# A transformer block on one core: order lists written out, tile 0's second centring behind tile 2's statistics, tile 1 copied by ScalarE alone

## The chip, the core and the metric

The kernel runs on one core of a Trainium2 chip. Its engines have queues of their own and meet through semaphores: TensorE (PE; its weight loads are PEld), VectorE (DVE), ScalarE (ACT), GpSimd (POOL) and SyncE (SP), which issues DMAs here. The metric is the device time of one execution in microseconds, the median of the runs; smaller is better.

## The reference

```python
x: (1, 2048, 512)   w1, w2: (512, 512)   w3: (512, 1792)   w4: (1792, 512)   all bf16
h   = gelu(layernorm(x) @ w1)              # tanh form
g0..g3 = the four 128-column quarters of h, shifted along the tokens
         by 1 down, 1 up, 2 down, 2 up, with zeros at the ends
x1  = x + concat(g0, g1, g2, g3) @ w2
out = x1 + gelu(layernorm(x1) @ w3) @ w4
```

## The kernel before

The 2048 tokens are 16 tiles of 128. A first layer (layernorm, w1, gelu) gives `hT`, transposed, with the tokens along the row, so that the shifted quarters are only other slices of it. `mix` multiplies them by w2 and adds x. A second layer (layernorm, w3, gelu, w4) gives the output. Everything stays on the chip between.

Each piece of work is an `Op` with a name, an engine and the resources that it reads and writes. Below, q is the tile for layer 1 and 16 + tile for layer 2:

- **Statistics** (lines 407 to 440). On VectorE `bnst` (batch-norm statistics of a tile, L432) and `bnag` (their aggregate, L434). For tiles in `STAT_ACT` ScalarE takes the sums instead (`sum`, L411, and `ssq`, L416; in layer 2 the sum falls out of the addition), and VectorE finishes with `mean`, `msq` (L424) and `vpe` (L428, which reads two small tensors). GpSimd then makes `rstd` (L439).
- **Normalizing**, `norm`: on VectorE (L461, from mean and rstd), or on ScalarE (L470) or GpSimd (L473), for which `nmr` (L466), minus mean times rstd, is made first. `NORM` chooses the engine, `NMR` that of nmr. Tile 0 is only centred (L448), in two halves `norm0_0` and `norm0_1`, and its rstd is applied later, inside its gelu.
- **Transposing.** Tiles 0 to 7 of layer 1 are transposed by TensorE (L506) and copied from PSUM to `xnT` (`ev`, L514); `EVAC` says by ScalarE, VectorE, or one half each ("both"). All others go through a DMA transpose that SP issues (`tp`, L479).
- **Matmuls.** `rows0` for tile 0 (L544) with `gelur0` and a transpose back, `th0`, copied by `evh0`; `up1` and `up2` (L642) for groups of 1, 2 or 4 tiles (`GROUPS`), in blocks of at most 1024 PSUM columns, each followed by a gelu on ScalarE (L657); `mix` (L697), followed by `x1`, the addition on VectorE (L709 or L713); `down` (L731), followed by `res` (L739) and the output's DMA.

PSUM is divided in two. `y_ps` is three pairs of banks, taken in turn by up, rows0 and the transposes called `ty` in the script. `o_ps` is two banks, taken in turn by mix, down, th0 and the transposes called `tp` in the script. A bank is taken again when its reader is done.

TensorE's order is the one of `SCRIPT` (lines 290 to 295). The other four engines' orders come out of a planner: `order()` works out a due time for each op from written-in costs (`dur`, `HOP`, `BIAS`), and `place()` plays the program through with them and lets each engine take the most urgent op that is ready. `LOADS` gives the order of the DMA loads and of two of the DMA transposes among them. `emit` (L811) writes the instructions and waits in that order; the ops planned ahead of 1900 ns stand ahead of the entry barrier.

The orders that came out, as far as 26 us, by engine:

```
SP    x0 x2 w1a w1b x3 x4 w2b w2a x6 x7 x8 w3 x12 x11 tp16 tp17 x14 tp9 tp8 tp10 tp11 tp12
ACT   sum0 ssq0 ev0_0 ev0_1 ev1act gelur0 sum5 gelu1_1 ssq5 gelu1_2 sum7 ev3 norm5 ssq7 gelu1_3 sum9 ev6act norm7 ...
DVE   bnst1 bnag1 norm0_0 norm0_1 bnst2 norm1 bnag2 msq0 vpe0 norm2 ev1dve bnst3 ev2 bnag3 bnst4 evh0 norm3 bnag4
      msq5 vpe5 bnst6 norm4 bnag6 x1_0 ev4 msq7 x1_1 ev5 vpe7 bnst16 ev6dve bnag16 bnst17 bnag17 norm16 x1_2 norm17
      msq9 vpe9 ev7 bnst8 x1_3 bnag8 bnst11 norm8 msq10 vpe10 bnag11 x1_5 nmr10 msq12 nmr11 vpe12 bnst13 bnag13 x1_4 ...
POOL  rstd1 rstd2 rstd0 rstd3 rstd4 rstd5 nmr5 rstd6 nmr6 norm6 rstd7 nmr7 rstd16 rstd17 rstd9 nmr9 norm9 rstd8 rstd10
      rstd11 norm10 rstd12 rstd13 nmr12 rstd15 nmr15 rstd14 norm15 ...
```

Of the kernel before, what the change touches and what calls it, by code (L numbers as in the profile page):

```python
# [6 lines left out]
P = 128  # L7
# [7 lines left out]
class Op:  # L15


    def __init__(self, name, eng, fn, reads, writes, dur, queue):
        self.name, self.eng, self.fn = name, eng, fn
        self.reads, self.writes = list(reads), list(writes)  # L20
        self.dur, self.queue = dur, queue
        self.idx = 0
        self.descs = 8.0
        self.prio = 1e9
        self.first = None

class Program:

    HOP = {"pe": 200.0, "dve": 155.0, "act": 220.0, "pool": 120.0, "sp": 70.0}
    LOOK = {"dve": 300.0, "act": 300.0}
    DUE = 179877.0
    BEGIN = {"sp": 30.0, "act": 150.0, "pe": 400.0, "dve": 150.0, "pool": 450.0}
    ENTRY = 1900.0
    COLD, RESTART = 4300.0, 800.0
    RING = 150.0
    LAG = {"load": 750, "tp": 350}

    def __init__(self):  # L40
        self.ops = []
        self.lines = []

    def add(self, eng, name, fn, reads=(), writes=(), dur=100.0, queue=None):
        op = Op(name, eng, fn, reads, writes, dur, queue)
        op.idx = len(self.ops)
        self.ops.append(op)
        return op

    def line(self, names):  # L50

        self.lines.append(list(names))

    def order(self):
# [25 lines left out]
        order_only = set()  # L80
        for names in self.lines:
            for a, b in zip(names, names[1:]):
                assert named[a].eng == named[b].eng, (a, b)
                order_only.add((named[a].idx, named[b].idx))
        last = None
        pe_pos = 0
        for op in self.ops:
            if op.eng == "pe":
                if last is not None:
                    preds[op.idx].add(last.idx)  # L90
                last = op
                op.prio = pe_pos
                pe_pos += 1
        order_only = {(a, b) for a, b in order_only if a not in preds[b]}
        for a, b in order_only:
            preds[b].add(a)
        succs = [set() for _ in self.ops]
        for i, d in enumerate(preds):
            for j in d:
                succs[j].add(i)  # L100
        left = [len(s) for s in succs]
        stack = [i for i, n in enumerate(left) if n == 0]
        seen = 0
        while stack:
            i = stack.pop()
            seen += 1
            for j in preds[i]:
                if self.ops[j].eng != "pe":
                    self.ops[j].prio = min(self.ops[j].prio, self.ops[i].prio)
                left[j] -= 1  # L110
                if left[j] == 0:
                    stack.append(j)
        assert seen == len(self.ops), "cycle"
        if self.DUE:

            topo, left = [], [len(d) for d in preds]
            stack = [i for i, n in enumerate(left) if n == 0]
            while stack:
                i = stack.pop()
                topo.append(i)  # L120
                for j in succs[i]:
                    left[j] -= 1
                    if left[j] == 0:
                        stack.append(j)
            due, t = {}, self.DUE
            for op in self.ops:
                if op.eng == "pe" and not op.name.startswith("warm"):
                    due[op.idx] = t
                    t += op.dur
            for i in reversed(topo):  # L130
                op = self.ops[i]
                late = due.get(i, 1e9)
                for j in succs[i]:
                    o = self.ops[j]
                    hop = 70.0 if op.queue else (self.HOP[op.eng] if o.eng != op.eng else 120.0)
                    work = (2300.0 if op.queue == "tp" else op.dur + 1850.0) if op.queue else op.dur
                    late = min(late, o.prio - hop - work)
                op.prio = late
        for op in self.ops:
            op.prio += BIAS.get(op.name, 0.0)  # L140
            if op.first is not None:
                op.prio = op.first
        for names in self.lines:
            for a, b in reversed(list(zip(names, names[1:]))):
                named[a].prio = min(named[a].prio, named[b].prio - 1e-3)

        self.preds = preds
        out = self.place(succs, order_only)
        for a, b in order_only:
            preds[b].discard(a)  # L150
        return out

    def place(self, succs, order_only):

        npend = [len(d) for d in self.preds]
        ready = [0.0] * len(self.ops)
        cands = {e: [] for e in ENGINES}
        for op in self.ops:
            if npend[op.idx] == 0:
                cands[op.eng].append(op)  # L160
        free = dict(self.BEGIN)
        rings = {"sp": [], "act": []}
        fed = {}
        clock = moved = last = turned = self.total = 0.0
        out = []

        def finish(limit):
            nonlocal clock
            while True:
                heads = {e: r[0] for e, r in rings.items() if r}  # L170
                if not heads:
                    return None
                live = [e for e in heads if heads[e][0] <= clock]
                later = min([h[0] for h in heads.values() if h[0] > clock], default=1e18)
                if not live:
                    if later > limit:
                        return None
                    clock = later
                    continue
                first = min(live, key=lambda e: heads[e][1])  # L180
                step = heads[first][1] * len(live)
                ends = clock + step <= min(later, limit)
                if not ends:
                    step = min(later, limit) - clock
                for e in live:
                    heads[e][1] -= step / len(live)
                clock += step
                if ends:
                    return rings[first].pop(0)[2]
                if clock >= limit:  # L190
                    return None

        def release(op, o, at):
            npend[o.idx] -= 1
            if at is not None:
                ready[o.idx] = max(ready[o.idx], at)
            if npend[o.idx] == 0:
                cands[o.eng].append(o)

        def land(op):  # L200
            nonlocal moved, last, turned
            if op.queue == "tp":
                turned = max(clock + 500.0, op.start + 2450.0, last + 500.0, turned + 480.0)
                at = turned + self.LAG["tp"]
            elif op.name.startswith("out"):
                at = clock + 300.0
                self.total = max(self.total, at)
            else:
                moved += op.dur
                at = clock + 600.0 + min(600.0, 0.3 * moved) + (600.0 if op.dur > 1400.0 else 0.0)  # L210
                at += 50.0 if moved <= 1200.0 else self.LAG["load"] - 300.0 if moved <= 4000.0 else self.LAG["load"] if moved <= 11000.0 else self.LAG["load"] + 650.0
            if op.queue != "tp":
                last = max(last, at)
            op.landed = at
            for j in succs[op.idx]:
                if (op.idx, j) not in order_only:
                    release(op, self.ops[j], at + 30.0)

        while len(out) < len(self.ops):
            while True:  # L220
                best = None
                for e in ENGINES:
                    if cands[e]:
                        t = max(free[e], min(ready[o.idx] for o in cands[e]))
                        if best is None or t < best[0]:
                            best = (t, e)
                op = finish(best[0] if best else 1e17)
                if op is None:
                    break
                land(op)  # L230
            t, e = best
            look = self.LOOK.get(e, 1.0)
            op = min((o for o in cands[e] if ready[o.idx] <= t + look), key=lambda o: (o.prio, o.idx))
            cands[e].remove(op)
# [674 lines left out]
```

## Time and profile before

| | |
|---|---|
| median of 3 runs | 135.43 us (134.98 to 135.43) |
| span of the profiled execution | 133.73 us from its first to its last instruction |
| its whole time, if it was a median run | 135.43 us: 1.70 us lie around the span |
| TensorE busy | 130.6 us, 98% |
| VectorE, ScalarE, GpSimd busy | 50.9, 56.0, 30.9 us |
| granted TensorE clock | 1.00 in all stretches |
| first transpose of tile 1 (tp1) | 5.12 us |
| first up2 block | 19.06 us |
| last matmul's result added | 131.96 us |
| DMA | 12.19 MB, mean 91 GB/s |

The page gives the busy time of each engine, then the span in 40 slices of 3.3 us, each with the busy share in tenths. The chain of work that ended last is followed back from the last instruction: its pieces say who set the time at each moment. The timeline lists instructions with start, length, engine, line and tiles. The starts of neighbouring instructions of one engine tell its pace better than their lengths do, since instructions overlap by a tenth of a microsecond.

### The profile page before, as it was taken

The numbers are of one execution on the slowest core, as the hardware profiler recorded it, in microseconds if no ns is written. First come the engines' busy times: TensorE is split into PE (matmuls) and PEld (weight loads), VectorE is DVE, ScalarE is ACT, GpSimd is POOL, SyncE is SP. The second block draws the span as 40 slices with busy tenths as digits, with TensorE's granted clock in tenths as the row PEclk, the third lists the DMA queues.
The fourth block names the chain that finished last, engine by engine and source line by source line (L and its number), as shares of the span: only waits on it lengthen the run. The fifth ranks groups of instructions, "written<-read, shape, count | busy, mean of one in ns | idle before, by whom it ended". The sixth has DMA issues, their size and how long they took to land.

```text
span 133.7 us, 2004 instructions
## 1 busy us (share of the span) xinstructions
PE 130.6 (98%) x776; PEld 71.8 (54%) x789; DVE 50.9 (38%) x138; ACT 56.0 (42%) x89; POOL 30.9 (23%) x69
## 2 busy tenths in 40 slices
PE   8999999999999999999999999999999999999994
PEld 3488768874488444444444444444444444444464
DVE  1899998887550830052260003322220000232223
ACT  5699998858657155520025553000006663000000
POOL 2447567696544120012022003100000000000000
PEclk9999999999999999999999999999999999999999
DMA  4999966745442991002211000311111000111112
GB/s 134 329 349 401 237 150 95 83 89 107 98 99 49 295 329 40 0 0 43 77 42 39 0 0 0 78 39 44 39 42 37 0 0 0 39 44 39 39 39 78
DMA packets 21305, 12.19 MB, mean 91 GB/s; under 512 B 13872, under 2 KB 20784, under 8 KB 21296
## 3 DMA queue, kind: packets, MB, share of 16 engines
q1 hardware_dynamic: 20864, 11.93, 32.7%
q10 hardware_dynamic: 432, 0.13, 0.4%
q8 instruction: 6, 0.10, 0.3%
q14 instruction: 3, 0.02, 0.1%
HBM read 6.82 MB, written 2.10 MB: 67 GB/s over the span
## 4 chain that ended last, share of the span: by engine, by line
PE 94%; DMA 2%; DVE 2%; issue 1%; SPq 0%
PE y_ps L642 46%; PE o_ps L731 36%; PE o_ps L697 10%; DMA x_sb<-in_x_dram 2%; PE y_ps L506 1%; DVE st L432 1%; PE y_ps L544 1%; DVE xn_buf L448 0%; DVE xn_buf L461 0%; DVE o_sb L739 0%; PE o_ps L610 0%; DVE mv L434 0%; SPq L894 0%
## 5 line engine op out<-in xcount | busy, mean ns | idle before, releaser
L642 PE MATMUL y_ps<-xnT,w_sb 128*128 128x512 bf16 (+2 forms) x421 | 63.6, 308 | 0.2
L642 PEld LDWEIGHTS y_ps<-xnT,w_sb 128*128 128x128 bf16 x424 | 38.4, 98 | 24.6 <-DVE mv L434 0.2
L731 PE MATMUL o_ps<-w_sb,h2T 128*128 128x512 bf16 (+3 forms) x248 | 48.7, 355 | 0.2
L657 ACT ACTIVATE h2T<-y_ps 128x1024 bf16<-128x1024 f32 (+1 forms) x29 | 28.6, 993 | 47.2 <-PE y_ps L642 47.1
L731 PEld LDWEIGHTS o_ps<-w_sb,h2T 128*128 128x128 bf16 x252 | 23.6, 98 | 25.2
L739 DVE TENSOR_TENSOR o_sb<-o_ps,x_sb 128x512 bf16<-128x512 f32 (+3 forms) x18 | 11.4, 632 | 45.7 <-PE o_ps L731 45.7
L439 POOL TENSOR_TENSOR rstd<-mv,neghalf 128x1 f32<-128x1 f32 x20 | 11.1, 553 | 35.1 <-DVE mv L434 30.1
L697 PE MATMUL o_ps<-w_sb,hT 128*128 128x512 bf16 x58 | 14.8, 379 | 0.3
L432 DVE BATCH_NORM_STATS2 st<-x_sb 128x6 f32<-128x512 bf16 x20 | 13.5, 676 | 2.6 <-DMA x_sb<-in_x_dram 2.5
L713 DVE TENSOR_TENSOR x_sb<-o_ps,x_sb 128x512 bf16<-128x512 f32 x10 | 6.8, 677 | 14.8 <-PE o_ps L697 14.8
L439 POOL TENSOR_TENSOR rstd<-vpe,neghalf 128x1 f32<-128x1 f32 x12 | 6.7, 558 | 15.6 <-DVE vpe L428 15.5
L473 POOL TENSOR_SCALAR xn_buf<-x_sb,rstd,nmr 128x512 bf16<-128x512 bf16 x12 | 9.2, 764 | 1.0 <-DVE nmr L466 0.4
L657 ACT ACTIVATE hT<-y_ps 128x512 bf16<-128x512 f32 (+1 forms) x10 | 8.1, 806 | 3.1 <-PE y_ps L642 2.9
L697 PEld LDWEIGHTS o_ps<-w_sb,hT 128*128 128x128 bf16 x64 | 6.1, 98 | 5.7
L709 DVE SCALAR_TENSOR_TENSOR x_sb<-o_ps,x_sb 128x512 bf16<-128x512 f32 x6 | 4.1, 681 | 12.1 <-PE o_ps L697 12.1
L416 ACT ACTIVATE junk<-x_sb 128x512 bf16<-128x512 bf16 x12 | 7.5, 622 | 2.1 <-DVE x_sb L709 2.0
L461 DVE TENSOR_SCALAR xn_buf<-x_sb,mv,rstd 128x512 bf16<-128x512 bf16 x13 | 6.1, 471 | 2.7 <-POOL rstd L439 2.0
L470 ACT ACTIVATE xn_buf<-x_sb,nmr,rstd 128x512 bf16<-128x512 bf16 x6 | 4.9, 813 | 0.5 <-POOL nmr L466 0.4
L756 PE MATMUL o_ps<-zeros 128*128 128x512 bf16 x9 | 4.0, 631 | 0.4 <-DVE zeros L363 0.4
L411 ACT ACTIVATE junk<-x_sb 128x512 bf16<-128x512 bf16 x6 | 3.7, 624 | 1.2 <-DMA x_sb<-in_x_dram 1.2
L434 DVE BATCH_NORM_AGGREGATE mv<-st 128x2 f32<-128x9 f32 x20 | 3.8, 192 | 0.3
L506 PE MATMUL y_ps<-ident,xn_buf 128*128 128x128 bf16 x32 | 3.4, 236 | 0.2 <-DVE xn_buf L461 0.2
(34 smaller groups left out, 28.7 us busy)
## 6 DMA issues: line engine op xcount, KB each, us to landing
out_dram<-o_sb SPq DMA_DIRECT2D x15, 128.0 KB, 1.7
w_sb<-in_w_dram SPq DMA_DIRECT2D x1, 1792.0 KB, 10.9
w_sb<-in_w_dram SPq DMA_DIRECT2D x2, 896.0 KB, 6.2
x_sb<-in_x_dram SPq DMA_DIRECT2D x4, 256.0 KB, 3.6
w_sb<-in_w_dram SPq DMA_DIRECT2D x4, 256.0 KB, 4.3
x_sb<-in_x_dram SPq DMA_DIRECT2D x5, 128.0 KB, 4.5
x_sb<-in_x_dram SPq DMA_DIRECT2D x1, 384.0 KB, 5.7
xnT<-xn_buf SPq DMA_TRANSPOSE x24, 2.5
```

The lines of the kernel that those rows point to most:

```text
L416: (lambda d: (lambda e: e.activation(d, src, ACT_F.Square, accum_out=sums[:, q, 1:2])))(junk[:, b, :]),
L432: pg.add("dve", f"bnst{q}", lambda e: e.bn_stats(st9[:, q, 0:6], src), reads=rs, writes=[(("st", q), 0)], dur=605)
L439: lambda e: e.tensor_tensor(col(rstd), var, neghalf[:], ALU.pow),
L461: lambda e: e.tensor_scalar(dst, src, mv[:, q, 0:1], rstd[:, q : q + 1], ALU.subtract, ALU.mult),
L470: f = lambda e: e.activation(dst, src, ACT_F.Identity, bias=nmr[:, q : q + 1], scale=rstd[:, q : q + 1])
L473: f = lambda e: e.tensor_scalar(dst, src, rstd[:, q : q + 1], nmr[:, q : q + 1], ALU.mult, ALU.add)
L642: ins = e.matmul(y_ps[:, p, W * i : W * (i + 1)], wsb[:, dc, P * fc : P * (fc + 1)], src[:, dc, P * t0 : P * t0 + W], start=(dc == 0), sto ...
L657: (lambda d, s: (lambda e: e.activation(d, s, ACT_F.Gelu_apprx_tanh)))(dst, ysrc),
L697: ins = e.matmul(dst, hT[:, j, c0 : c0 + P], w2_sb[:, j, :], start=(j == order[0]), stop=(j == order[-1]))
L713: f = lambda e: e.tensor_tensor(x1_sb[:, t, :], dst, x_sb[:, t, :], ALU.add)
L731: ins = e.matmul(dst, h2T[:, fc, P * t : P * (t + 1)], w4_sb[:, fc, cs], start=(fc == 0), stop=(fc == FC - 1))
L739: (lambda d, c: (lambda e: e.tensor_tensor(o_sb[:, oi, c], d, x1_sb[:, t, c], ALU.add)))(dst, cs),
```

## The change

The planner goes. Each engine but TensorE gets its order written out in `ORDER`, TensorE's `SCRIPT` is a new one, and the tables that choose an engine for each norm, copy and statistic are new. The `dur` of every op, which only the planner used, goes too. The arithmetic, the groups of tiles, the number of matmuls and of transposes, the tiles transposed by TensorE, the three pairs and two banks and the split of the last tile (`TAIL`) stay.

What changes in the order:

- Start: VectorE does bnst1 bnag1 norm0_0 **bnst2 norm0_1 bnag2** norm1, where it did bnst1 bnag1 norm0_0 norm0_1 bnst2 norm1 bnag2. Tile 1's transposes go to an o_ps bank (`tp:1`, it was `ty:1`), and ScalarE alone copies them.
- Tiles 3, 4, 5, 7 and 8: norm3 moves from VectorE to ScalarE, norm4 from VectorE to GpSimd, norm5 and norm7 from ScalarE to GpSimd, norm8 from VectorE to GpSimd; norm6 moves from GpSimd to VectorE. tp4 and tp6 use o_ps banks. tp7 stands ahead of up1:5.
- mix4, mix5 and mix6 stand together ahead of the first up2 block; before it was mix5 and mix4, and mix6 after up1:7.
- up2 is a step for each block (`up2:0.4` is group 0's block from column block 4), and the blocks are mixed with up1, mix and down.
- SP: x11 and x12 go ahead of w3, x14 behind it, and all DMA transposes come after x14.
- STAT_ACT has 9 tiles where it had 12; ScalarE's passes over x for statistics are 14 where they were 18.
- The four `junk` buffers, where ScalarE's statistics put what nobody reads, are taken in ScalarE's own order.
- AHEAD names the ops ahead of the entry barrier; they are the same ones.

The diff, cut to its core:

```diff
-NORM = {5: "act", 6: "pool", 7: "act", 9: "pool", 10: "pool", 11: "act", 12: "act", 15: "pool", 18: "act", 19: "pool", 20: "act", 21: "pool", 23: "pool", 25: "pool", 26: "pool", 28: "pool", 30: "pool", 31: "pool"}
-EVAC = {1: "both", 2: "dve", 4: "dve", 5: "dve", 6: "both", 7: "dve", 8: "dve", 9: "dve", 10: "dve", 13: "dve", 14: "both", 16: "both", 18: "dve", 21: "dve", 28: "dve", 29: "both", 30: "both", 31: "both"}
-STAT_ACT = (0, 5, 7, 9, 10, 12, 19, 21, 23, 24, 25, 31)
+NORM = {3: "act", 4: "pool", 5: "pool", 7: "pool", 8: "pool", 11: "act", 12: "act", 13: "act", 15: "act", 17: "pool", 18: "pool", 19: "act", 21: "act", 22: "pool", 23: "pool", 27: "pool", 29: "pool", 31: "act"}
+EVAC = {0: "act", 1: "act", 2: "both", 3: "both", 4: "act", 5: "dve", 6: "dve", 7: "act"}
+STAT_ACT = (0, 7, 9, 10, 12, 17, 20, 21, 28)
 LOADS = """
-x0-1 x2 tp2 w1a w1b x3 x4-5 w2b w2a tp5 x6 tp6 x7 x8-10 tp4 w3 x12-13 tp0 x11 tp17 x14-15 tp26 tp5 w4a tp3
-w4b
+x0-1 x2 w1a w1b x3 x4-5 w2b w2a x6 x7 x8-10 w3 x12-13 x11 x14-15 w4a w4b
 """
 SCRIPT = """
-warm:9 sa:0 sb:0 ty:1 ra:0 rb:0 ty:2 up1:1 th:0 up1:2 mix:0 ty:3 mix:1 ty:4 up1:3 ty:5 up1:4 ty:6 mix:2
-up1:5 ty:7 mix:3 up1:6 mix:5 mix:4 up2:0 up1:7 mix:6 up1:8 mix:7-8 up1:9 mix:10 mix:9 up2:1 mix:13 mix:11
...
+warm:9 sa:0 sb:0 tp:1 ra:0 rb:0 ty:2 up1:1.0 th:0 up1:2.0 mix:0 ty:3 mix:1 tp:4 up1:3.0 ty:5 up1:4.0 tp:6
+mix:2 ty:7 up1:5.0 mix:3 up1:6.0 mix:4 mix:5 mix:6 up2:0.0 up2:0.4 up1:7.0 up2:0.8 mix:8 up1:8.0 mix:7
+up2:0.12 mix:10 mix:9 up1:9.0 up1:9.2 up2:1.0 mix:14 mix:11 up2:1.4 up2:1.8 mix:13 mix:12 up2:2.0 up2:2.2
+up2:2.4 up2:1.12 mix:15 up2:2.6 up2:2.8 up2:2.10 down:0 down:2 up2:3.0 down:1 up2:2.12 up2:3.2 up2:3.4 down:3
...
 """
+ORDER = {
+    "sp": """
+dma_x0 dma_x2 dma_w1a dma_w1b dma_x3 dma_x4 dma_w2b dma_w2a dma_x6 dma_x7 dma_x8 dma_x11 dma_x12 dma_w3
+dma_x14 tp16 tp17 tp8 tp9 tp11 tp10 tp15 tp13 tp14 tp12 tp19 tp18 tp20 tp23 tp24 tp25 tp22 tp26 tp21 dma_w4a
...
+""",
+    "act": """
+warm_gelu sum0 ssq0 ev0_0 ev0_1 ev1 gelur0 ev2act gelu1_1_0 norm3 gelu1_2_0 ssq7 ev3act sum7 ev4 gelu1_3_0
+ssq17 sum9 ssq12 gelu1_4_0 ev7 sum10 ssq9 gelu1_5_0 gelu1_6_0 sum12 ssq10 ssq20 ssq21 norm11 norm19 gelu2_0_0
...
+""",
+    "dve": """
+zeros bnst1 bnag1 norm0_0 bnst2 norm0_1 bnag2 norm1 msq0 vpe0 norm2 bnst3 ev2dve bnag3 bnst4 bnag4 evh0 bnst5
+bnag5 bnst6 x1_0 ev3dve bnag6 x1_1 mean17 msq7 vpe7 msq17 norm6 ev5 bnst16 ev6 bnag16 vpe17 bnst8 x1_2 norm16
+bnst18 bnag8 bnag18 msq10 bnst11 bnag11 nmr18 msq9 x1_3 vpe9 bnst19 x1_4 norm9 mean20 bnag19 msq20 vpe20 x1_5
+mean21 msq21 bnst15 norm20 vpe10 vpe21 nmr19 x1_6 bnag15 bnst22 nmr21 bnag22 msq12 vpe12 bnst13 norm10 bnag13
+bnst14 nmr22 bnag14 x1_8 norm14 bnst24 bnag24 norm24 x1_7 bnst23 bnag23 x1_9 bnst25 x1_10 bnst26 bnag25 bnag26
...
+""",
+    "pool": """
+trip0 trip1 neghalf ident0 epsc pad0 ident1 pad1 rstd1 rstd2 rstd0 rstd3 nmr3 rstd4 nmr4 norm4 rstd5 nmr5
+norm5 rstd6 rstd7 nmr7 norm7 rstd16 rstd17 nmr17 norm17 rstd18 rstd8 nmr8 norm8 rstd9 rstd11 nmr11 rstd20
+norm18 rstd19 rstd21 rstd10 rstd15 rstd22 nmr15 rstd13 rstd12 nmr13 nmr12 rstd14 norm22 rstd24 rstd23 nmr23
...
+""",
+}
```

`order()` now takes each engine's next listed op as soon as the ops that it depends on have been written out, and keeps each list's order.

## The prediction

> **What bounds the kernel now.** I read the page's busy shares first, then the slices, then the chain of work that ended last, and last the timeline around the steps that the change reorders. The busy shares and slices of four engines:
>
> ```profile
> PE 130.6 (98%) x776; PEld 71.8 (54%) x789; DVE 50.9 (38%) x138; ACT 56.0 (42%) x89; POOL 30.9 (23%) x69
> ...
> PE   8999999999999999999999999999999999999994
> ...
> DVE  1899998887550830052260003322220000232223
> ACT  5699998858657155520025553000006663000000
> POOL 2447567696544120012022003100000000000000
> ```
>
> TensorE is full from the second slice to the last but one. The helpers are full in the first eight slices (27 us) and light afterwards: trouble can arise there and hardly later. The chain says the same with times (start, length, what):
>
> ```profile
> 2.87 0.70 DVE st L432
> ...
> 3.80 0.36 DVE xn_buf L448 x2
> 4.15 0.60 DVE st L432
> 4.75 0.33 DVE xn_buf L461
> 5.08 0.05 issue
> 5.12 0.49 PE y_ps L506 x4
> ```
>
> Up to 5.12 VectorE sets the pace; from there on the chain is TensorE, with pieces of 0.05 "issue", up to the last addition at 131.96. I set the start of each group of matmuls in the trace against its number of matmuls at their closest spacing (0.216 us per 512 columns, 0.109 per 256, 0.056 per 128): of 126.8 us, some 0.2 are gaps. The change issues the same matmuls and transposes, so it can gain 0.2 us behind 5.12, and ahead of it only if VectorE frees norm1 earlier. Whatever makes TensorE wait is added whole. So I follow the new lists up to 36 us, asking at each TensorE step which input is last.
>
> **Part 1, the start: +0.10.** VectorE's rows:
>
> ```profile
> 3.71 0.44 DVE L448 TENSOR_SCALAR xn_buf<-x_sb,mv 128x256 bf16<-128x256 bf16 x2
> 4.07 0.68 DVE L432 BATCH_NORM_STATS2 st<-x_sb 128x6 f32<-128x512 bf16 x1
> 4.67 0.39 DVE L461 TENSOR_SCALAR xn_buf<-x_sb,mv,rstd 128x512 bf16<-128x512 bf16 x1
> 4.99 0.18 DVE L434 BATCH_NORM_AGGREGATE mv<-st 128x2 f32<-128x9 f32 x1
> 5.09 0.17 DVE L424 TENSOR_SCALAR mv<-mv 128x1 f32<-128x1 f32 x1
> ```
>
> norm0_1 goes from ahead of bnst2 to behind it; both stay ahead of norm1, so that costs norm1 nothing. New ahead of norm1 is bnag2, whose slot is 0.10 (4.99 to 5.09). norm1 and tp1 come 0.10 later. tp0_1 is 0.6 late, but only the second half of rows0 needs it, at 5.94, and its copy ends near 5.6. Tile 1's copy on ScalarE alone (598 ns, against halves that ended at 6.45) ends at 6.36; up1:1 asks at 6.64: free, cover 0.28. tile 2's half then ends at 7.66 behind gelur0 for 7.70: free, barely. norm2 is ready 0.3 earlier, but TensorE is still in rows0: no gain.
>
> **Part 2, GpSimd becomes the feeder: +0.21 and +0.09.** Tiles 4, 5 and 7 are now normalized on GpSimd; before, of the first eight only tile 6 was. Its pace:
>
> ```profile
> 9.39 0.55 POOL L439 TENSOR_TENSOR rstd<-vpe,neghalf 128x1 f32<-128x1 f32 x1
> 10.04 0.26 POOL L466 TENSOR_SCALAR nmr<-mv,rstd 128x1 f32<-128x1 f32 x1
> ...
> 11.00 0.26 POOL L466 TENSOR_SCALAR nmr<-mv,rstd 128x1 f32<-128x1 f32 x1
> 11.37 0.76 POOL L473 TENSOR_SCALAR xn_buf<-x_sb,rstd,nmr 128x512 bf16<-128x512 bf16 x1
> ```
>
> rstd to nmr takes 0.65, nmr to norm 0.37, norm to the next 0.75, nmr to a next rstd 0.23 (33.71 to 33.94). The new list is rstd3 nmr3 rstd4 nmr4 norm4 rstd5 nmr5 norm5. rstd3 waits for bnag3, which now stands behind ev2dve: tile 2's transposes are out at 6.80, ev2dve starts at 6.90, bnag3 runs from 7.11 to 7.30. From rstd3 at 7.38: rstd4 8.26, norm4 9.29, rstd5 10.04, norm5 11.06 to 11.82; tp5 can start at 11.88. TensorE is there at 11.67 (11.56, the chain's 11.78 less 0.22 of pipeline, plus 0.10): **+0.21**. Before, ScalarE had norm5 done at 11.26. Next: rstd6 11.81, rstd7 12.33, nmr7 12.98, norm7 13.35 to 14.11, tp7 at 14.17. TensorE runs tp5, up1:4, tp6 and mix2 in 0.22+0.89+0.22+0.86 and asks at 14.07, with tp7 now ahead of up1:5: **+0.09**. Queued behind each are all later matmuls. mix1 and tp4 meet their inputs (gelu1_2 at 9.64; x1_0, which now frees tp4's bank, at 10.46) within 0.1: I take nothing, the range holds 0.1 each.
>
> **Part 3, three mixes on two banks: +0.20.** mix4, mix5 and mix6 now stand together, and there are two o_ps banks, so mix6 waits for x1_4 to empty mix4's. Before, never more than two stood together. The lag, weight load of a mix to its addition:
>
> ```profile
> 42.66 1.50 PEld L697 LDWEIGHTS o_ps<-w_sb,hT 128*128 128x128 bf16 x8
> ...
> 43.83 0.69 DVE L713 TENSOR_TENSOR x_sb<-o_ps,x_sb 128x512 bf16<-128x512 f32 x1 [4.97 <-PE o_ps L697]
> ```
>
> 1.17 + 0.69 + 0.06 to restart is 1.92; two mixes take 1.73: **+0.20**, with VectorE idle at the right moment. mix4 starts at 17.89 (tp7 14.17 +0.22, up1:5 1.75, mix3 0.86, up1:6 0.89), so x1_4 could start at 19.06.
>
> **Part 4, vpe9 behind norm8: +0.42.** VectorE is not idle there. From norm6 (rstd6's end 12.36, so 12.39), by slots of 0.60 for statistics (0.69 where the aggregate follows at once), 0.60 to 0.64 for an addition, 0.31 for a norm, 0.33 for a copy and 0.08 to 0.13 for small ones, the list reaches x1_3 at 17.66, vpe9 at 18.26, bnst19 at 18.35 and x1_4 at 18.95: just in time. But GpSimd's norm8 (bnag18 out 16.58, rstd18 16.66, rstd8 17.18, nmr8 17.83) runs from 18.20 to 18.96, and the trace has this:
>
> ```profile
> 20.34 0.76 POOL L473 TENSOR_SCALAR xn_buf<-x_sb,rstd,nmr 128x512 bf16<-128x512 bf16 x1
> ...
> 20.57 0.53 DVE L428 SCALAR_TENSOR_TENSOR vpe<-sums,mv 128x1 f32<-128x1 f32 x1
> ...
> 21.03 0.68 DVE L432 BATCH_NORM_STATS2 st<-x_sb 128x6 f32<-128x512 bf16 x1
> ```
>
> A vpe of 159 ns by its median took 528 and ended with the norm; norms of 413 ns took 0.80 and 0.87 beside such norms, while additions and statistics there kept their length. So vpe9 ends at 18.96, bnst19 starts at 18.89, x1_4 at 19.49, and mix6 goes at 20.24, not 19.81: **+0.42**. A hold of ev6 (13.63, inside norm7) is in no row; bounds 0 and +0.2 on VectorE; I take 0.
>
> [...]
>
> **Part 5, what costs nothing.** SP: x11 and x12 now lead w3, 0.38 MB, so w3 (issued 5.54, 10.9 to landing: 16.5) lands 1.1 later at its own rate of 1.8 MB in 5.7 us, and x14 near 18.3; tp16 and tp17 stand behind x14 and land by 19.7 (norm17 ends at 16.40, 1.3 a transpose, 2.5 to landing); up2:0 asks at 21.1. In exchange no load stands among the transposes. tp10 (behind norm10) lands about 0.2 ahead of up1:8, tp12 (1.3 a transpose behind norm14) 0.05 ahead of up1:9. ScalarE does 14 statistics passes where it did 18, and two more norms: it is late nowhere ahead of TensorE. The split up2 blocks keep three y_ps pairs and a gelu of 1.02 per 1.73 of matmul; the tail is the same. Cover gone, each of these costs 0.1 to 0.5: they are the range's top.
>
> **Sum.** 0.10+0.21+0.09+0.20+0.42 = 1.02. The profiled execution's span is 133.73 and 1.70 lies around it if it was a median run (135.43 of 134.98 to 135.43): **136.4**.
>
> **Rivals.** (a) **vpe9 slips in first**, so not slower. vpe9 is due 0.06 behind norm8's start. If VectorE is 0.06 earlier or GpSimd later, vpe9 runs unheld and Part 4 is nothing: +0.60, 136.0, inside 0.5% (0.68 us, about what a measurement of this kernel can tell from no change). For it: the margin is smaller than my error. Against it: any VectorE delay up to 0.7 keeps vpe9 inside. (b) **Transposes late**: tp10 or tp12 miss by 0.4 to 0.9: 136.8 to 137.3. For: the 0.05. Against: a later TensorE gives them time. (c) **Clock**: the warm-ups stand 0.43 apart, the rows' matmuls 0.216, tp0's 0.107 and tp1's 0.063: full speed comes between 4.6 and 5.1. If the emptier stretch of 4.4 to 5.2 put it off by another 3.8 us, as long as the warm-ups ran slow, half of that is lost on top of the sum: 138.3. [...] (d) **The lists hold no stall**: each chain is some 0.1 to 0.3 shorter than my slots and the additions hide: 135.2 to 135.6; its best is the 0.2 of gaps. Against: Part 3 is measured lags only.
>
> **Numbers.** Forecast 0.40 (136.2 to 136.8), (a) 0.33, (b) 0.11, (c) 0.02, (d) 0.14. Slower by over 0.5%: 0.40, (b), (c) and 0.05 of (a), 0.58; within: 0.28 of (a), 0.10 of (d), 0.38; faster: 0.04. The range leaves out (c) and the far ends of (b) and (d): 135.4 to 137.2.
>
> **What would show it.** tp1 near 5.23; TensorE gaps ahead of tp5 and tp7, released by GpSimd's norm; a gap of 0.2 (rival a) or 0.6 ahead of mix6, released by VectorE's addition; a vpe near 18.3 of 0.15 or 0.7 us. Wrong would be a TensorE without gaps up to 21 us, or gaps ahead of up1:8 and up1:9, released by a DMA.

## The result, and the profile after

| | before | after |
|---|---|---|
| median | 135.43 us (6 runs, 134.98 to 135.61) | 136.66 us (6 runs, 136.13 to 137.14) |
| profiled execution | span 133.73 | 136.13, span 134.80 |
| TensorE, VectorE, ScalarE, GpSimd busy | 130.6, 50.9, 56.0, 30.9 us | 131.6, 49.3, 54.7, 29.3 us |

The changed kernel is slower by a ratio of 1.0102, 95% interval [1.0078, 1.0126]. The forecast was 136.4 in 135.4 to 137.2: the time fits, but not for the reasons given. These are the busy shares and the slices of the page of after:

```profile
PE 131.6 (98%) x776; PEld 71.4 (53%) x789; DVE 49.3 (37%) x132; ACT 54.7 (41%) x85; POOL 29.3 (22%) x67
...
PE   8999999999999999999999999999999999999994
...
DVE  1899997947728511610320022001200303012222
ACT  5689985997250546540233044353000340530000
POOL 2569896871430630400000000000000000000000
PEclk9999999999999999999999999999999999999999
```

These lines say little: TensorE is as full as before and the other engines do less. PEclk reads full from the first slice on, where the warm-ups stand 0.427 us apart and not 0.216, so neither it nor the 1.00 in the table of before can speak on rival (c). A loss of 1 us on TensorE is spread over 40 slices. So I put TensorE's completions against its own pace, as in the prediction: for each step the time from the completion before it to its own, less its matmuls at the closest spacing. What is left over, behind tp1, is listed by the step that stood still (us; the column rows0 is time lost there to the late load of w1b or, where said, to a slow pace; every kernel has 0.1 to 0.2 more in pieces under 0.04):

| profiled execution | rows0 | tp5, tp7 | mix6 or up2:0 | mix8, up1:8, up1:9 | up2:2 |
|---|---|---|---|---|---|
| before | 0 | 0 | 0 | 0 | 0 |
| after | 0.37 | 0.10 | 0.11 | 0.34 | 0 |

Of the whole, 0.16 in before and 1.08 in after. The start comes on top: tp1 at 5.17, before 5.12, and tp1's four transposes take 0.61, before 0.49. The chain of waits of after, up to 8 us (start, length, what):

```profile
2.85 0.70 DVE st L270
...
3.77 0.16 DVE xn_buf L286
3.93 0.60 DVE st L270
4.53 0.20 DVE xn_buf L286
4.73 0.05 issue
4.78 0.39 PE y_ps L343 x2
5.17 0.61 PE o_ps L343 x4
```

Against before's, the two half centrings (before one piece of 0.36 ahead of the statistics) stand around tile 2's statistics, and TensorE does tp0_1 at 4.78 before it comes to tp1 at 5.17. The four matmuls of rows0 in after, by twos, and the load of the third one's weights:

```profile
5.57 1.01 PE L380 MATMUL y_ps<-w_sb,xnT 128*128 128x512 bf16 x2
6.41 0.60 PE L380 MATMUL y_ps<-w_sb,xnT 128*128 128x512 bf16 x2
```

```profile
6.11 0.10 PEld L380 LDWEIGHTS y_ps<-w_sb,xnT 128*128 128x128 bf16 x1 [0.39 <-DMA w_sb<-in_w_dram]
```

The first two matmuls complete 0.427 and 0.373 us behind the step before each, the other two 0.216. tp1's transposes, too, complete 0.107 apart, where 0.056 is full pace. So TensorE ran at half pace, that of the warm-ups, until about 6.4 us; in before's profiled execution it did so until about 5.4 (the prediction read 4.6 to 5.1). The late load of w1b cost nothing in after: the third matmul's weights were in at 6.21, and it began at 6.41, when the second let it. (At full pace that load would have held it in the pace's place, by some 0.2; an estimate from before_1, where the third matmul began 0.05 behind the load's landing.) The event of rival (c) thus did happen, by 1.0 us and not by 3.8, which was an estimate from how long the warm-ups ran slow. It cost 0.37 at rows0 and 0.11 at tp1, 0.48 of the 1.07 by which the two spans differ. That the change put it off is not shown: in again, the same kernel, full pace came near 3.7 us (see the last section). Next the timeline of after from 26.5 us, TensorE (start, length, engine, line, operation; in brackets the idle time and what ended it), at the first two late steps beyond 21 us, mix8 and up1:9:

```profile
28.26 0.81 PE L530 MATMUL o_ps<-w_sb,hT 128*128 128x512 bf16 x3 [0.22 <-ACT hT L491]
...
34.28 1.89 PE L476 MATMUL y_ps<-xnT,w_sb 128*128 128x512 bf16 x8
```

mix8 waits for a gelu of ScalarE. up1:9 starts at 34.28, right behind tile 12's transpose by DMA, which lands at 34.19. Both lie beyond the 21 us in which I put every loss.

### The profile page after: what moved, and what is told of

The parts are those of the page before. It is cut to its first block, busy times and chain, and to the rows that moved or that the text cites. A ratio compares the mean times of both kernels' runs of the same rounds, so it can differ in the third digit from the quotient of the medians.

```text
span 134.8 us, 1981 instructions
## 1 busy us (share of the span) xinstructions
PE 131.6 (98%) x776; PEld 71.4 (53%) x789; DVE 49.3 (37%) x132; ACT 54.7 (41%) x85; POOL 29.3 (22%) x67
## 4 chain that ended last, share of the span: by engine, by line
PE 94%; DMA 2%; DVE 2%; issue 1%; SPq 0%
PE y_ps L476 46%; PE o_ps L564 36%; PE o_ps L530 10%; DMA x_sb<-in_x_dram 2%; PE y_ps L343 1%; DVE st L270 1%; PE y_ps L380 1%; PE o_ps L343 1%; DVE xn_buf L286 0%; DVE o_sb L572 0%; PE o_ps L445 0%; DVE mv L272 0%; SPq L714 0%
## 5 line engine op out<-in xcount | busy, mean ns | idle before, releaser
L476 PE MATMUL y_ps<-xnT,w_sb 128*128 128x512 bf16 (+2 forms) x420 | 65.0, 308 | 0.2
L277 POOL TENSOR_TENSOR rstd<-mv,neghalf 128x1 f32<-128x1 f32 x23 | 12.6, 552 | 24.0 <-DVE mv L272 17.2
L270 DVE BATCH_NORM_STATS2 st<-x_sb 128x6 f32<-128x512 bf16 x23 | 15.7, 682 | 3.1 <-DMA x_sb<-in_x_dram 2.9
L546 DVE TENSOR_TENSOR x_sb<-o_ps,x_sb 128x512 bf16<-128x512 f32 x12 | 8.2, 686 | 9.4 <-PE o_ps L530 9.4
L310 POOL TENSOR_SCALAR xn_buf<-x_sb,rstd,nmr 128x512 bf16<-128x512 bf16 x10 | 7.7, 773 | 1.2 <-DVE nmr L303 0.4
L254 ACT ACTIVATE junk<-x_sb 128x512 bf16<-128x512 bf16 x9 | 5.6, 620 | 3.6 <-DVE x_sb L542 3.6
L307 ACT ACTIVATE xn_buf<-x_sb,nmr,rstd 128x512 bf16<-128x512 bf16 x8 | 6.3, 807 | 0.2 <-DVE nmr L303 0.2
L277 POOL TENSOR_TENSOR rstd<-vpe,neghalf 128x1 f32<-128x1 f32 x9 | 4.9, 547 | 1.2 <-DVE vpe L266 1.1
L303 POOL TENSOR_SCALAR nmr<-mv,rstd 128x1 f32<-128x1 f32 x13 | 3.6, 277 | 0.9
L249 ACT ACTIVATE junk<-x_sb 128x512 bf16<-128x512 bf16 x5 | 3.1, 624 | 1.1 <-DMA x_sb<-in_x_dram 1.1
L542 DVE SCALAR_TENSOR_TENSOR x_sb<-o_ps,x_sb 128x512 bf16<-128x512 f32 x4 | 2.7, 687 | 0.4 <-PE o_ps L530 0.3
```

The costliest lines, as they stand in the source:

```text
L254: (lambda d: (lambda e: e.activation(d, src, ACT_F.Square, accum_out=sums[:, q, 1:2])))(junk[:, b, :]),
L270: pg.add("dve", f"bnst{q}", lambda e: e.bn_stats(st9[:, q, 0:6], src), reads=rs, writes=[(("st", q), 0)])
L277: lambda e: e.tensor_tensor(col(rstd), var, neghalf[:], ALU.pow),
L307: f = lambda e: e.activation(dst, src, ACT_F.Identity, bias=nmr[:, q : q + 1], scale=rstd[:, q : q + 1])
L310: f = lambda e: e.tensor_scalar(dst, src, rstd[:, q : q + 1], nmr[:, q : q + 1], ALU.mult, ALU.add)
L476: ins = e.matmul(y_ps[:, p, W * i : W * (i + 1)], wsb[:, dc, P * fc : P * (fc + 1)], src[:, dc, P * t0 : P * t0 + W], start=(dc == 0), sto ...
```

## The experiments

The kernels are the changed kernel with edits in its lists, and twice the kernel before. Times of runs on different chips are compared by their ratio to the kernel before on the same chip.

**The changed kernel again, and three edits alone.**

again: no edit. start_back, VectorE:

```diff
-norm0_0 bnst2 norm0_1 bnag2 norm1
+norm0_0 norm0_1 bnst2 norm1 bnag2
```

mix6_later, TensorE, and vpe9_inside, VectorE:

```diff
-mix:4 mix:5 mix:6 up2:0.0 up2:0.4
+mix:4 mix:5 up2:0.0 mix:6 up2:0.4
...
-msq9 x1_3 vpe9
+x1_3 msq9 vpe9
```

> The changed kernel as it is, for a second trace and more times. In its first trace TensorE lost 1.04 us more than before between tp1 and up1:9: 0.43 at rows0, whose second half waited for the load of w1b (6.07, against 5.52 before); 0.16 at mix6; 0.20 at mix8, behind gelu1_7; 0.13 at up1:9, behind tp12; the rest at tp5. vpe9 began 0.02 ahead of norm8 and was not held. Theory A (the new lists feed TensorE late; where the loss shows depends on what comes first): again 136.4 to 137.0, with 1.0 to 1.5 us of gaps in all, but at other places: if w1b lands by 5.7, no gap at rows0 and a gap of about 0.2 ahead of tp5, and if vpe9 falls behind norm8's start, a vpe of up to 0.7 us and a gap of about 0.6 ahead of mix6. Theory B (the loss is the late w1b, and the lists are as good as before): with w1b by 5.7 the gaps behind tp1 are 0.6 us and the time is 136.0 or less; with w1b late, as in the first trace.

> The start alone undone: VectorE does norm0_0 norm0_1 bnst2 norm1 bnag2 as before, all else as changed. Theory A: tp1 starts 0.07 to 0.10 earlier, and the feeding chain on GpSimd with it; time 0.1 below the changed kernel, not to be told from it by 5 rounds. Theory B's variant, in which the start is what the change costs: rows0 and all behind it come 0.5 earlier and the time is 0.4 to 0.6 below the changed kernel.

> mix6 behind the first up2 block, so that never more than two mixes stand together. Theory A: the gap ahead of mix6 (0.15, or 0.6 where vpe9 is held) is gone, since an up2 block of 1.74 us gives x1_4 its time; up2:0 then asks for tp17 0.9 earlier, near 20.0, about when it lands, so that 0 to 0.2 comes back there; time 0.1 to 0.5 below the changed kernel, more where the hold is frequent. Theory B (two banks are no bound; the gap is frame or noise): no change of time, and mix4, mix5, then up2:0 show the same gap.

> VectorE does x1_3 msq9 vpe9 where it did msq9 x1_3 vpe9, so that vpe9 comes about 0.24 later, inside norm8 (which began 0.02 behind it in the first trace and takes 0.77). If such a vpe is held until GpSimd's norm ends: vpe9 takes 0.4 to 0.6 us instead of 0.15, x1_4 starts about 0.55 later than without, and the gap ahead of mix6 is 0.6 to 0.8 us; time 0.4 to 0.6 above the changed kernel as its first trace has it, less above its median if that is held in some runs too. If it is not held: vpe9 takes 0.16, the gap is 0.3, time at most 0.15 above.

| kernel | median, us | ratio to before | rows0 | tp5, tp7 | mix6 or up2:0 | mix8, up1:8, up1:9 | up2:2 |
|---|---|---|---|---|---|---|---|
| again | 136.40 | 1.0069 [1.0045, 1.0094] | 0.31 | 0.15 | 0.11 | 0.33 | 0 |
| start_back | 136.52 | 1.0080 [1.0063, 1.0097] | 0.30 | 0.15 | 0.11 | 0.31 | 0.81 |
| mix6_later | 136.95 | 1.0101 [1.0080, 1.0121] | 0.27 | 0.26 | 0.12 | 0.34 | 0.70 |
| vpe9_inside | 136.61 | 1.0078 [1.0058, 1.0098] | 0.33 | 0.16 | 0.12 | 0.33 | 0.49 |

(In mix6_later w2b's load, too, held a mix up: that is most of its 0.27. In vpe9_inside 0.03 of the 0.33 is half pace.) None of the three edits makes the kernel faster. What each shows by itself:

- start_back: from x0's landing to tp1 it is 2.27 us, as in before, against 2.35 in after and again. Part 1 is 0.075.
- mix6_later: mix6 no longer waits, but up2:0 now comes early and waits 0.12 for tile 17's transpose, which lands at 19.96. The 0.11 of three mixes can't be had here.
- vpe9_inside: vpe9 began 0.10 inside GpSimd's norm8 and was not held. VectorE and GpSimd in its timeline:

```profile
18.73 0.16 DVE L266 SCALAR_TENSOR_TENSOR vpe<-sums,mv 128x1 f32<-128x1 f32 x1
```

```profile
18.64 0.76 POOL L310 TENSOR_SCALAR xn_buf<-x_sb,rstd,nmr 128x512 bf16<-128x512 bf16 x1
```

- A loss that no theory had: up2:2, 0.5 to 0.8 in these three and none in after and again. TensorE in start_back:

```profile
44.74 1.67 PE L530 MATMUL o_ps<-w_sb,hT 128*128 128x512 bf16 x7
47.06 1.24 PE L476 MATMUL y_ps<-xnT,w_sb 128*128 128x512 bf16 x5 [0.65 <-ACT h2T L491]
```

The row names ScalarE, but that gelu had long ended: up2:2's last input is tp21, last of nineteen transposes that SP issues up to there, which lands between 46.8 and 47.0 in these three. In after and again it landed at 46.0 to 46.1.

**The kernel before, twice more.** Two theories on the 0.3 of w1b: that the change moved other transfers into its way, or chance.

> The kernel before, for another trace. In its first trace w1b landed at 5.52, in five traces of the changed lists at 5.95 to 6.42, where TensorE lost 0.3 to 0.4 us at rows0 or mix0 for it. The first twelve DMAs are the same ones in the same order in both. If the load's landing is chance of the run (theory B'), w1b lands between 5.4 and 6.4 here and TensorE loses what it is late behind 5.7; the before's first trace was then a lucky one, and its median time holds some 0.3 of this loss too. If it belongs to the change (theory A'), it lands at 5.4 to 5.6 again and there are no gaps behind tp1.

> As before_1, a third trace of the kernel before: theory B' 5.4 to 6.4, theory A' 5.4 to 5.6.

135.44 and 135.20 us, one run each. The kernel before can lose the same time in the same place: 0.36 in the first and 0.02 in the second (w1b landed at 6.18 and 5.88; in the first profile of before at 5.52, with no loss). TensorE of before_1:

```profile
5.45 0.59 PE L544 MATMUL y_ps<-w_sb,xnT 128*128 128x512 bf16 x2
6.23 0.61 PE L544 MATMUL y_ps<-w_sb,xnT 128*128 128x512 bf16 x2 [0.19 <-DMA w_sb<-in_w_dram]
```

So a late load is not the change's alone. That it is no more frequent with the change is not shown: w1b landed at 5.95 to 6.42 in all eleven profiles of the changed lists, and earlier than that in two of the three of the kernel before. The profile of after, for which the expectation of again names this load, is no case of it: its loss at rows0 is the half pace above.

**tp21 earlier, bnag3 earlier.** SP and VectorE:

```diff
-tp23 tp24 tp25 tp22 tp26 tp21
+tp23 tp22 tp21 tp24 tp25 tp26
...
-bnst3 ev2dve bnag3
+bnst3 bnag3 ev2dve
```

> SP issues tp21 and tp22 right behind tp23, ahead of tp24 to tp26, which are wanted 18 us later. In three of five traces of the changed lists TensorE lost 0.5 to 0.8 at up2:2's first block, where tp21 landed at 46.8; in the other two it landed at 46.0 and nothing was lost. If these three are what separates the slow half of the changed kernel's runs (136.5 to 137.1) from its fast half (136.0 to 136.4), then here tp21 lands near 43.5, no gap stands ahead of up2:2, and the times are 135.9 to 136.4 with a median 0.2 to 0.5 below the changed kernel's; the gaps at tp5, mix6, mix8 and up1:9 stay, 0.1 to 0.2 each. If the spread has another cause, the times go from 136.0 to 137.1 as before.

> VectorE aggregates tile 3 (bnag3) ahead of its half of tile 2's copy (ev2dve), not behind it; nothing else moves. In six traces of the changed lists ev2dve waited for TensorE's tp2 and bnag3, and with it GpSimd's chain rstd3 to norm5 to norm7, stood behind that wait by 0.3 us; tp5 then cost 0.04 to 0.20 and tp7 0.06. If GpSimd's chain is what tp5 and tp7 wait for: rstd3 starts 0.3 to 0.4 earlier, norm5 ends as much earlier, both gaps are below 0.03, and the time falls by 0.1 to 0.25 if VectorE and the DMAs behind it don't give it back (mix6 0.11, mix8 0.17, up1:9 0.13 and up2:2 0 to 0.8 stay). If those gaps belong to TensorE's change from 512 to 128 columns and not to the wait, they stay and the time is unchanged.

tp21_early: 136.13 us (12 runs), 1.0048 [1.0025, 1.0070]. up2:2's gap is gone; TensorE goes straight on behind the mixes:

```profile
44.84 1.67 PE L530 MATMUL o_ps<-w_sb,hT 128*128 128x512 bf16 x7
46.35 1.89 PE L476 MATMUL y_ps<-xnT,w_sb 128*128 128x512 bf16 x8
```

The rest of its losses are those of again, but for a smaller one at rows0. One of the twelve runs still took 137.14, so that tp21 is not all of the spread. tp21's place thus costs some 0.3 us in the mean (1.0048 against again's 1.0069; the intervals overlap), 0 to 0.8 in a profiled execution.

bnag3_first: 136.78 us, 1.0101 [1.0065, 1.0138]. A miss. rstd3 came 0.2 earlier, but rstd4 waits for bnag4, bnag4 for bnst4, and that for bnst3, which waits for x3's load (6.53); norm5 ran from 11.31 to 12.08 and tp5 still lost 0.16. Its executions are three near 136.2 and three near 137.4. tp21 stands where it stood and may be what parts them, but the profile is of a run of the first kind.

**vpe9 inside norm8.** Two memsets of scratch that nothing reads push vpe9 back, of 128 columns (vpe9_deep) and of 512 (vpe9_deeper):

```diff
-msq9 x1_3 vpe9
+x1_3 msq9 spare0 spare1 vpe9
```

> In vpe9_inside vpe9 began 0.10 into norm8 and took 0.16: not held. The vpe of the first profile that took 0.53 began 0.24 into a norm on GpSimd. Here two spare memsets of 128 columns stand ahead of vpe9, so that it begins 0.3 to 0.45 into norm8 (they write a scratch tile that nothing reads). [...] If a vpe isn't held at all: 0.16, and the gap is that of vpe9_inside plus the memsets' time, about 0.3 to 0.4.

> As vpe9_deep, where vpe9 began only 0.13 into norm8 and took 0.13, with spare memsets of 512 columns instead of 128, so that it begins 0.25 to 0.6 into norm8. The vpe that took 0.53 in all three traces of the kernel before began 0.24 into a norm. [...] If not held: 0.13 to 0.16 long, and the long one before has another cause.

vpe9_deep: 135.99 us in its one run; vpe9 began 0.13 inside norm8 and took 0.13: not held. vpe9_deeper: 136.81 us in its one run. Its VectorE, then GpSimd, then TensorE:

```profile
19.02 0.25 DVE L269 SCALAR_TENSOR_TENSOR vpe<-sums,mv 128x1 f32<-128x1 f32 x1
19.20 0.68 DVE L273 BATCH_NORM_STATS2 st<-x_sb 128x6 f32<-128x512 bf16 x1
19.80 0.67 DVE L545 SCALAR_TENSOR_TENSOR x_sb<-o_ps,x_sb 128x512 bf16<-128x512 f32 x1
```

```profile
18.51 0.77 POOL L313 TENSOR_SCALAR xn_buf<-x_sb,rstd,nmr 128x512 bf16<-128x512 bf16 x1
```

```profile
20.54 1.04 PE L533 MATMUL o_ps<-w_sb,hT 128*128 128x512 bf16 x4 [0.46 <-DVE x_sb L545]
```

Here vpe9 begins 0.51 inside and ends within 0.01 of the norm's end (19.28), 0.25 in place of 0.15. The addition x1_4 comes 0.55 later than in after and mix6 loses 0.63. That is near the 0.62 of Parts 3 and 4 together, but not by Part 4's mechanism: vpe9 begins 0.54 later than in after because of the memsets, and the hold adds 0.10 to its length. The run shows that a hold exists and that a VectorE late by 0.55 costs mix6 as much; a hold of 0.55 at vpe9, the price of Part 4, occurred in no run.

**All repairs together.**

mended: the edits of start_back, bnag3_first, mix6_later and tp21_early; vpe10 ahead of vpe20, norm10 behind nmr19 and rstd10 behind nmr11, all earlier; and on ScalarE

```diff
-norm11 norm19 gelu2_0_0 gelu2_0_4 norm15 gelu1_7_0
+norm11 gelu2_0_0 norm19 gelu2_0_4 norm15 gelu1_7_0
```

> All the waits that the traces named, mended at once in the changed lists: VectorE's start as before, bnag3 ahead of ev2dve, mix6 behind the first up2 block, tp22 and tp21 ahead of tp24, gelu2_0_0 ahead of norm19 on ScalarE, and tile 10 earlier (vpe10 and norm10 on VectorE, rstd10 on GpSimd), so that the transposes for up1:9 start earlier. If the account of the loss is complete, TensorE loses behind tp1 only what w1b or w2 are late (0 to 0.36, as the kernel before does too) and up to 0.15 elsewhere, and the time is that of the kernel before within 0.3 us: 135.2 to 135.8. If more than 0.4 us stay, a part of the loss has a cause that was not found.

136.14 us, 1.0055 [1.0042, 1.0069]; expected were 135.2 to 135.8. The gaps at up1:9 and up2:2 are gone, tp5 keeps 0.13 and tp7 0.06, up2:0 0.08, and mix8 has 0.48 where it had 0.17. ScalarE and TensorE of mended:

```profile
26.38 0.81 ACT L307 ACTIVATE xn_buf<-x_sb,nmr,rstd 128x512 bf16<-128x512 bf16 x1 [0.44 <-POOL nmr L303]
27.10 1.00 ACT L491 ACTIVATE hT<-y_ps 128x1024 bf16<-128x1024 f32 x1
```

```profile
28.16 0.61 PE L530 MATMUL o_ps<-w_sb,hT 128*128 128x512 bf16 x2 [0.30 <-ACT hT L491]
```

My edit made ScalarE wait 0.44 for GpSimd's nmr15 with gelu1_7 behind it, and mix8 behind gelu1_7. One repair pushed the next feeder back.

mended_2: as mended, but norm5 and norm15 on VectorE, without their nmr:

```diff
-norm11 gelu2_0_0 norm19 gelu2_0_4 norm15 gelu1_7_0
+norm11 gelu2_0_0 norm19 gelu2_0_4 gelu1_7_0
...
-bnag6 x1_1 mean17 msq7 vpe7
+bnag6 norm5 x1_1 msq7 vpe7 mean17
...
-nmr21 bnag22 msq12
+nmr21 bnag22 norm15 msq12
```

> All the repairs so far together, and two feeders moved: the start as in the kernel before (norm0_1 ahead of bnst2, bnag2 behind norm1), bnag3 ahead of ev2dve, mix6 behind the first up2 block, tp22 and tp21 ahead of tp24 on SP, norm5 and norm15 on VectorE, gelu1_7 right behind gelu2_0_4 and ahead of norm19, vpe10, norm10 and rstd10 earlier. Theory (the loss is the sum of TensorE's gaps, and each gap is a late feeder in the written lists): the gaps at tp5 and at mix8 are gone (norm5 ends near 11.3 instead of 12.1, gelu1_7 starts near 26.3), at most 0.12 stays at mix6 or the first up2 block, 0 to 0.2 at up1:9, none at the third up2 group; behind tp1 TensorE loses at most 0.4 us beyond what the late w1b load costs. Time 135.4 to 135.9, 0 to 0.4 above the kernel before. Rival (the new order of the matmuls itself costs, whatever feeds it: other pairings of banks, weights switched more often): the gaps go, and more than 0.5 us stays.

(gelu1_7 stands behind norm19, not ahead of it as this has it.)

136.60 us, 1.0106 [1.0090, 1.0122]; expected were 135.4 to 135.9. The gaps at tp5, mix8, up1:8, up1:9 and up2:2 are gone, as expected; tp7 keeps 0.06. But up2:0 lost 1.13 us:

```profile
20.65 1.58 PE L476 MATMUL y_ps<-xnT,w_sb 128*128 128x256 bf16 x13 [0.96 <-DMA xnT<-xn_buf]
```

That DMA is tp17. The trace's DMA view, first over the stretch that holds tp17's issue alone, then from 19.0 to 19.5 us (the last line: issues, and their median us to landing):

```profile
xnT<-xn_buf SPq DMA_TRANSPOSE x1, 3.5
```

```profile
q14 instruction: 1, 0.01, 3.9%
```

In mended the same transpose, over the same kind of stretch, has no instruction packet in its flight:

```profile
xnT<-xn_buf SPq DMA_TRANSPOSE x1, 2.5
```

So the gap does not come from the order of the lists: an instruction packet fell into tp17's flight (19.08 us; tp17 was issued at 16.98). In after that packet comes at 22.56. vpe9_deep and vpe9_deeper, which like mended_2 have two VectorE instructions more than after, have it at 19.05 and 19.39, and tp17 took 3.4 us in both; there mix6 stood ahead of up2:0 and hid it. That the matmuls' order costs by itself (the rival) is not borne out: in its profile every piece of mended_2's loss has a late feeder with a name, and without the 1.13 its median would be some 135.5, an estimate that takes every run to have it; that lies within the range expected. But a version of the new order that reaches the kernel before was not found; the closest is tp21_early, 1.0048. The losses of these runs, as in the tables above (0.09 of vpe9_deeper's 0.17 at rows0 is half pace):

| kernel | rows0 | tp5, tp7 | mix6 or up2:0 | mix8, up1:8, up1:9 | up2:2 |
|---|---|---|---|---|---|
| tp21_early | 0.15 | 0.14 | 0.11 | 0.31 | 0 |
| bnag3_first | 0.26 | 0.22 | 0.11 | 0.35 | 0 |
| vpe9_deep | 0.18 | 0.16 | 0.11 | 0 | 0.49 |
| vpe9_deeper | 0.17 | 0.19 | 0.63 | 0 | 0.45 |
| mended | 0.27 | 0.19 | 0.08 | 0.48 | 0 |
| mended_2 | 0.29 | 0.06 | 1.13 | 0 | 0 |

## Why the time was right, and the reasons only in part

- **Part 1**, 0.10 for bnag2's slot: 0.075 measured (start_back). Right.
- **Part 2**, GpSimd the feeder. The chain is as worked out. GpSimd in after, tile 3's rstd, then norm5, then norm7:

```profile
7.74 0.55 POOL L277 TENSOR_TENSOR rstd<-mv,neghalf 128x1 f32<-128x1 f32 x1 [1.69 <-DVE mv L272]
...
11.37 0.76 POOL L310 TENSOR_SCALAR xn_buf<-x_sb,rstd,nmr 128x512 bf16<-128x512 bf16 x1
...
13.63 0.76 POOL L310 TENSOR_SCALAR xn_buf<-x_sb,rstd,nmr 128x512 bf16<-128x512 bf16 x1
```

```profile
12.19 0.40 PE L343 MATMUL y_ps<-ident,xn_buf 128*128 128x128 bf16 x4
```

  4.39 us from rstd3 to norm5's end (12.13), 4.44 predicted. tp5 (the last row) and tp7 wait for it, but lose 0.04 and 0.06, not 0.21 and 0.09. TensorE itself was about 0.5 later at tp5 than the sum had it, by the half pace, and norm5's end 0.31 later (predicted 11.82), so that little of the 0.21 was left. Over the runs tp5's loss is 0.04 to 0.20 (0.20 in mix6_later). With norm5 on VectorE and bnag3 early (mended_2) tp5's is gone. Right in kind, mis-sized by 0.2.
- **Part 3**, 0.20: 0.11. From mix4's first weight load (18.14) to mix6's (20.01) it took 1.87; 1.92 was predicted. Right in kind. mix6's weights in after wait for VectorE's addition:

```profile
18.14 1.45 PEld L530 LDWEIGHTS o_ps<-w_sb,hT 128*128 128x128 bf16 x8
20.01 0.55 PEld L530 LDWEIGHTS o_ps<-w_sb,hT 128*128 128x128 bf16 x4 [0.42 <-DVE x_sb L542]
```

- **Part 4**, 0.42: nothing. This is the step that failed, and rival (a) took its place by its own mechanism. VectorE and GpSimd around 18.5 us in after:

```profile
18.48 0.15 DVE L266 SCALAR_TENSOR_TENSOR vpe<-sums,mv 128x1 f32<-128x1 f32 x1
18.60 0.70 DVE L270 BATCH_NORM_STATS2 st<-x_sb 128x6 f32<-128x512 bf16 x1
19.25 0.69 DVE L542 SCALAR_TENSOR_TENSOR x_sb<-o_ps,x_sb 128x512 bf16<-128x512 f32 x1
```

```profile
18.50 0.78 POOL L310 TENSOR_SCALAR xn_buf<-x_sb,rstd,nmr 128x512 bf16<-128x512 bf16 x1
```

  vpe9 was due 0.06 behind norm8's start, and comes 0.02 ahead of it. The prediction added that any delay of VectorE up to 0.7 keeps vpe9 inside and held; at 0.10 and 0.13 inside it wasn't held, at 0.51 it was. In before, vpe12 began 0.24 inside norm10 and was held in each of three profiles (0.53 us). So in these few cases a vpe that began up to 0.13 behind the norm's start was not held, and one that began 0.24 or more behind it was; what holds it, no run shows. ev6, whose hold the prediction took as 0, began 0.3 inside norm7 and took 0.41 where ev5 took 0.42: not held.
- **Part 5**, nothing for the transposes and ScalarE: 0.34 at mix8, up1:8 and up1:9, in after, and as much in all the runs above but the two with spare memsets and the two repaired ones, and 0 to 0.8 at up2:2. tp12's cover of 0.05 was a loss of 0.13 at up1:9 (rival b in its place, smaller than its price of 0.4 to 0.9). A gap there, released by a DMA, is what the prediction named as a sign that it is wrong. mix8 hangs on ScalarE, which I called late nowhere: VectorE's x1_5 begins at 21.38 with 0.30 of idle time that no input explains (mix5's result was there at 20.09), and behind it come, on ScalarE, ssq21, norm11, norm19, two gelus, norm15 and gelu1_7. x1_5, and ScalarE's ssq21 waiting for it:

```profile
21.38 0.69 DVE L542 SCALAR_TENSOR_TENSOR x_sb<-o_ps,x_sb 128x512 bf16<-128x512 f32 x1 [0.30 <-PE o_ps L530]
```

```profile
22.11 0.63 ACT L254 ACTIVATE junk<-x_sb 128x512 bf16<-128x512 bf16 x1 [1.30 <-DVE x_sb L542]
```

  tp21 I did not judge at all: I followed the lists to 36 us, because the helpers looked light behind 27, and it is due at 46. SP is in no slice of the page.
- **The time around the span**, 1.70: 1.33 in after, 1.35 in before_1 and before_2. The profiled execution of before was no median run but one of about 135.1. The predicted span was 134.75, and 134.80 came out, but with other terms: 0.05 of start, 0.21 of Parts 2 and 3, 0.34 of Part 5, and 0.48 of half pace at tp1 and rows0, which no run ties to the change. Of the 1.02 that the prediction added up, 0.26 came by its own reasons. Part 4's 0.42 did not come at all, and losses that the prediction put at nothing, or left to a rival, stood in its place: that the time was right is luck. The median of after lies 0.5 above its profiled execution; some 0.3 of that may be tp21, by tp21_early, and the rest is open.
- **The sums redone**: 14.17 less 14.07 is 0.10, not 0.09 (tp7), 20.24 less 19.81 is 0.43, not 0.42 (Part 4), and 0.38 MB at 1.8 MB in 5.7 us is 1.2, not 1.1 (w3). None of it changes the forecast.

One point stays open: what held x1_5 for 0.30. In mended, with one more VectorE instruction ahead of it, the gap stands one instruction earlier in the work (vpe20 waits 0.67 where it waited 0.32) and x1_5 follows at once; in vpe9_deep, with two more, there is none and mix8 loses nothing. vpe9_deeper and mended_2 have none either, and these three are the kernels whose instruction packet comes at 19.05 to 19.39 and not at 22.3 to 22.6. That looks like a place in the instruction stream and not like an input, but no run tested it by itself.

## What to carry to other kernels

Where an engine is 98% full, add up its gaps step by step from its completions, to the end of the program and not only where the helpers look busy, and take the queue of DMA issues as a helper with a pace of its own: the step due last in a run of back-to-back transposes is the one that showed a delay in it (tp21, 0.8 to 1.0 late behind tp26's slow issue). Put the first steps' spacing against the full pace before a loss there is given to an input: a matmul that runs slowly and one that waits look alike in a sum of completions (0.37 at rows0 in after, 0.36 in before_1). A term that hangs on 0.06 us of order between two engines is a coin, and both of its sides belong in the sum. Repairing one feeder moved the next (mix8's loss went from 0.17 to 0.48 in mended); when a repair "does nothing", look for the gap that came in its place before giving up the theory of it.

## What the runs showed of the hardware

**Transposes took longer with an instruction packet in their flight.** Over the fourteen profiles, of the transposes that SP issued in the first 45.5 us, 203 had no instruction packet under way in the stretch from 1.1 to 2.7 us behind their issue: 2.50 us to landing in the median, 195 of them between 2.40 and 2.75 (the others stand behind a large load or a late one). 64 had one: 57 of these took 3.06 to 4.58 us; in the other seven the packet came 2.18 us or more behind the issue. The packets are of 8 and 16 KB and take 0.3 to 1.7 us. tp22 in start_back is one, in flight at the packet of 42.70; the DMA view, first over its issue alone, then from 42.0 to 43.5 us, with the next transpose:

```profile
xnT<-xn_buf SPq DMA_TRANSPOSE x1, 4.3
```

```profile
q8 instruction: 1, 0.02, 4.9%
...
xnT<-xn_buf SPq DMA_TRANSPOSE x1, 3.5
```

In the profiles of after, again and bnag3_first SP's issue of tp26, right behind it, takes 1.27 us, as usual, and tp21 lands at 46.0 to 46.1; in those of start_back, mix6_later and vpe9_inside that issue takes 2.0 to 2.3, and tp21 lands 0.8 to 1.0 later. That is up2:2's gap. What decides between the two is not shown: the packet begins 0.72 behind tp26's issue in again and 0.70 in start_back. In the three kernels with two more VectorE instructions a packet that falls at 22.3 to 22.6 in the other changed ones falls at 19.05 to 19.39, and in one of them, mended_2, up2:0 lost 1.13 us behind tp17, which took 3.5 us to landing. Whether an engine waited for such a packet is not shown here; a DMA transpose beside it took 0.6 to 2.1 us more.

**Loads vary from run to run.** w1b's landing was between 5.52 and 6.18 us in three profiles of the one kernel before, and TensorE's loss with it, 0 to 0.36: as much as the change's own terms.

**TensorE's full pace comes at another time in each run.** In all fourteen profiles the first matmuls of 512 columns complete 0.427 us apart and the later ones 0.216. The step between the two, read from the completions, came near 3.4, 5.3 and 5.4 us in the three profiles of the kernel before, and between 3.4 and 6.4 in the eleven of the changed lists. In seven of the fourteen it came during the warm-ups, which are the same in all. Where it came later, it came at 5.3 and 5.4 with the start as before and at 5.3 to 6.4 with the new one, so that a delay by the emptier stretch is neither shown nor excluded.
